# Gate and value by 15 products per 3 x 2 x 3 blocks instead of 7 per 2 x 2 x 2, in a Mamba2 scan with a SwiGLU layer

## The chip, the cores and the metric

One core of a Trainium2 chip runs the whole computation in one launch. The metric is device microseconds of an execution, median of the runs; lower is better. The engines are named as in the profile: PE (TensorE, matrix products; PEld is its weight load), DVE (VectorE), ACT (ScalarE), POOL (GpSimd) and SP (SyncE), whose queue issues nearly all DMAs. Tiles lie in SBUF, or in PSUM where PE writes its products.

## What is computed

A Mamba2 scan over 4 batches x 8 heads x 768 tokens (head width 32, state 16), whose output, as 3072 tokens x 256 features, goes through an RMS norm and a SwiGLU layer with 1536 hidden features. Everything is float32; the weights come as 64-bit floats.

```python
L = np.exp(cum[:, :, :, None] - cum[:, :, None, :]) * causal   # per chunk of 32 tokens
y_intra = np.einsum('bhij,bhjd->bhid', CB * L, xc)
y_inter = np.einsum('bhin,bhnd->bhid', Cc, state) * decay_to_i
...
xn = x / rms * rms_g                 # 3072 x 256
g, val = xn @ w_gate, xn @ w_val     # 256 -> 1536
out = (g / (1 + np.exp(-g)) * val) @ w_out
```

Written as products of 128 x 128 weights with 256 tokens, gate and value are 2 x 12 x 2 x 12 = 576 products; the output projection is half as much.

## The kernel before

The order of all work is written out by hand as one long string of steps; each step (`2:P.7.0` is step `P` of block 2 with arguments 7 and 0) issues a few instructions, every engine takes its instructions in that order, and an engine waits where an input is not there or a buffer is not free. So the string sets both the queues and what is behind a wait.

The tokens are cut into six blocks of 512 (`TB`). For each block the scan runs on pairs of 128-token chunks: B and C are transposed (`turn`, `T`, `Tt`), decays are spread by DMA (`spread`), shifted on DVE (`sub`, L467), exponentiated on ACT and masked on POOL (`ex`, L473 and L475), multiplied with the products of C and B (`g`, `L`), and give `y` with the carried states (`A`, `S`). The decays of the first four pairs are instead made on PE (`mask`, `sums`, L426 to L447). Then come the squares, the norm (`ms`, `rs`, `rb`, `xn`), and the layer.

The weights are brought in 20 pieces (`fetch`) and turned from 64-bit to 32-bit floats by ACT (`pow`) and DVE (`man`, `wt`: L192, L195, L201). All this work lies in the first 100 us, mixed with block 0, of which the first six feature tiles are computed by plain products (L827, L837).

The other gate and value products go by Strassen's scheme in its Winograd form: two feature tiles x two halves of the 256 inputs x two token halves of 256, 7 products instead of 8, for gate and value side by side in one bank. `combine_w` (`sw`, L881) and `combine_x` (`tx`, L888) make the sums of weights and of tokens; `product_gv` (L911) issues the products, 1, 6, 7, 4 onto the bank `gate` and 2, 5, 3 onto `val`; after 1, 6 and 7 ACT takes out the running sum (`take`, L917, tile `p`), and DVE adds it to `val` (`C`, L923, tile `c`). ACT applies SiLU (`silu`, L932) and DVE multiplies by the value (`hid`, L936) into the hidden tile `h`. The order string runs several pairs of feature tiles side by side.

The projection uses the same scheme on `h` and `w_out`: sums of `h` (`s`, `s3`, `s2`, `s4`; L967 to L977), sums of the weights (`two`, L957), products of 128 columns over all six feature pairs (`O`, L1001), `Otake` on ACT, `Oadd` on DVE (L1025, L1028), and the store. Block 0 is projected by plain products of 256 columns (L943).

Of the kernel before, what the change touches and what calls it, by code (L numbers as in the profile page):

```python
# [20 lines left out]
def kernel(  # L21
# [13 lines left out]

# [11 lines left out]
    NPAIR = T // 256  # L66
    TB = 512
    NT = TB // P
    NBLK = T // TB
# [4 lines left out]
    raw = ctx.enter_context(tc.tile_pool(name="raw", bufs=3))  # L74
    ssd = ctx.enter_context(tc.tile_pool(name="ssd", bufs=2))
    cvt = ctx.enter_context(tc.tile_pool(name="cvt", bufs=2))
    nrm = ctx.enter_context(tc.tile_pool(name="nrm", bufs=2))
    ffn = ctx.enter_context(tc.tile_pool(name="ffn", bufs=2))
    mm = ctx.enter_context(tc.tile_pool(name="mm", bufs=1, space=bass.MemoryType.PSUM))
    dram = ctx.enter_context(tc.tile_pool(name="dram", bufs=1, space=bass.MemoryType.DRAM))  # L80
    ctx.enter_context(tc.manual_schedule())
# [20 lines left out]

    pairs, later, sides = {}, {}, ("left", "right")
# [9 lines left out]
    def load(p, queues=(nc.sync, nc.sync)):  # L113
        b, c0 = divmod(2 * p, NC)
        br = raw.tile([P, 2, NH, N], FP32, tag="br", name="br")
        cr = raw.tile([P, 2, NH, N], FP32, tag="cr", name="cr")
        st.setdefault(p, {}).update(B=br, C=cr)
        for i in range(2):
            sl = slice((c0 + i) * P, (c0 + i + 1) * P)
            for dst, src in ((br, B), (cr, C)):  # L120
                queues[i].dma_start(out=dst[:, i], in_=src[b, :, sl, :].rearrange("h s n -> s h n"))  # L121

    def load_x(p, queue=nc.sync):
        b, c0 = divmod(2 * p, NC)
        st.setdefault(p, {})["x"] = raw.tile([P, 2, NH, D], FP32, tag="xr", name="xr")
# [5 lines left out]
    wgv = const.tile([P, 2, 2, DF], FP32, name="wgv")  # L131
    wg, wv = wgv[:, 0], wgv[:, 1]
    wo = const.tile([P, NF, DM], FP32, name="wo")

    def words(w):
# [7 lines left out]
    wdst = {"g": wg, "v": wv, "o": wo}  # L143
    pieces = [(n, c, w) for c, w in [(0, 128), (128, 128)] + [(c, 256) for c in range(256, DF, 256)]
              for n in "gv"]
    pieces += [("o", c, 2) for c in range(0, NF, 2)]
    fetched = {}

    def fetch(*ks):
        for k in ks:  # L150
            n, c, w = pieces[k]
            if n == "o":
                src, dst, shape = wsrc[n][:, c:c + w], wo[:, c:c + w], (w, DM)
            else:
                src, dst = wsrc[n][:, :, 2 * c:2 * (c + w)], wdst[n][:, :, c:c + w]
                shape = (2, w)
            small = shape[0] * shape[1] == 256
            r = raw.tile([P, shape[0], 2 * shape[1]], I32, tag="ws" if small else "wr",
                         name="wr", bufs=4 if small else 6)
# [6 lines left out]

    parts = {}

    def power(k):
        words16, (lo, hi), dst, shape = fetched[k]
        n = shape[1] * shape[2]
        e = cvt.tile([P, n], FP32, tag="e", name="e", bufs=4)
# [10 lines left out]
    def mantissa(k):  # L189
        words16, (lo, hi), dst, shape = fetched[k]  # L190
        m = cvt.tile(shape, I32, tag="m", name="m")
# [6 lines left out]
    def weight(k):  # L198
        words16, (lo, hi), dst, shape = fetched[k]
        e, f = parts.pop((k, "e")), parts.pop((k, "f"))  # L200
        nc.vector.scalar_tensor_tensor(out=dst, in0=f, scalar=2.0 ** -20, in1=e,  # L201
                                       op0=ALU.mult, op1=ALU.mult)

    a_sb = ffn.tile([BH, S], FP32, tag="ob", name="a_sb", bufs=1)
# [25 lines left out]
    early = nrm.tile([P, NC * BH + 2 * NG * NH], FP32, tag="xn", name="early", bufs=1)  # L230
# [128 lines left out]
    def three_parts(k):  # L359
        r_ps = ps.pop(("r", k))  # L360
        first = nrm.tile([P, 2, P], BF16, tag="first", name="first", bufs=1)
        nc.vector.tensor_copy(out=first, in_=r_ps)
        rest = nrm.tile([P, 2, P], FP32, tag="rest", name="rest", bufs=1)
        nc.vector.scalar_tensor_tensor(out=rest, in0=first, scalar=later_part, in1=r_ps,
                                       op0=ALU.mult, op1=ALU.add)
        second = nrm.tile([P, 2, P], BF16, tag="second", name="second", bufs=1)
# [46 lines left out]
    def pair_tile(g):  # L413
        p = g // 2
        if p not in Ls and p < 4:
            Ls[p] = ssd.tile([P, 2, NH, P if p < 2 else HC], FP32, tag="L", name="L", bufs=2)
        elif p not in Ls:
            Ls["of", p // 2] = L = ssd.tile([P, 4, NH, HC], FP32, tag="L", name="L", bufs=2)
            for k in range(2):
                Ls[p - p % 2 + k] = L[:, 2 * k:2 * k + 2]  # L420
# [61 lines left out]
    def scale(p):  # L482
# [3 lines left out]
        for name, src, d in (("Cd", "C", to_i), ("Bd", "B", from_j))[0 if p < 2 else 1:]:  # L486
            s[name] = ssd.tile([P, 2, NH, N], FP32, tag=name, name=name)
# [4 lines left out]
    def transposed(p):  # L492
        s = st[p]
        if "T" not in s:
            s["T"] = ssd.tile([P, 2, 4, P], FP32, tag="T", name="T")
        return s["T"]

# [29 lines left out]
    def spread_decays(p):  # L527
        b, c0 = divmod(2 * p, NC)
        st.setdefault(p, {})["dT"] = d = ssd.tile([P, 2, P], FP32, tag="Cd", name="dT")
# [5 lines left out]
    def turned_decayed(p):  # L535
        nc.vector.tensor_tensor(out=transposed(p)[:, :, 3], in0=ps["t", p][:, 1], in1=st[p]["dT"],
# [9 lines left out]
    def turned_last(p, copy):  # L546
        copy(out=transposed(p)[:, :, 3], in_=ps.pop(("t", p)))
# [31 lines left out]
    def products_of_block(blk, g):  # L579

        ps["g", blk] = gs = [g[:, 0], g[:, 1], bank("g2", (P, 512)), bank("g3", (P, 512))]
        ps["g pair", blk] = g
        for k in range(2):
            product(2 * blk + k, [(q, gs[q][:, 256 * k:256 * k + 256]) for q in range(NQ)], k == 0)

    def decayed_block(blk, q=None):

        L = Ls["of", blk]
        if q is None:
            L = L[:, :, 0:4].rearrange("p j (q t) m -> p q j (t m)", t=2)  # L590
            g = ps["g pair", blk].rearrange("p q (j m) -> p q j m", j=4)
        else:
            L = L[:, :, 2 * q:2 * q + 2].rearrange("p j t m -> p j (t m)")
            g = ps["g", blk][q].rearrange("p (j m) -> p j m", j=4)
# [39 lines left out]
    def states(p):  # L634
        A_ps = ps.pop(("A", p))
        b, c0, chunks = chunks_of(p)
        new = ssd.tile([P, 2, 2, 2, D], FP32, tag="A", name="A")
# [6 lines left out]
        for i, u in chunks:  # L644
            g, c = 2 * p + i, c0 + i
            S = ssd.tile([P, 2, D], FP32, tag="S", name="S", bufs=10)
# [9 lines left out]
    yts, sqs = {}, {}  # L656

    def first_outputs(p, y):
# [4 lines left out]
        def inter(i, opens):  # L663
            S, CdT = state[2 * (2 * p + i) - 1], s["T"][:, i, 3]
# [24 lines left out]
    def outputs(p, pair, after, n=0):  # L689
# [6 lines left out]
        width = 1 if p < 4 else 2  # L696

# [6 lines left out]
        for i in range(2):  # L704
            for u in range(2):
                for q in range(NQ):
                    if (2 * p) % NC == 0 and i == 0 and u == 0:
# [5 lines left out]
                              rhs=s["T"][r, i, 3, halves[u]], tile_position=(32 * q, o))  # L713
# [7 lines left out]
        for k, p2 in enumerate(after):  # L721
            cols = slice((width + n + k) * P, (width + n + k + 1) * P)
            additions(p2, [y[u][:, cols].rearrange("p (i t d) -> p i t d", i=2, t=2)
                           for u in range(2)])
        del st[p], Ls[p]

    def parts_of_y(p):
        y, n = ps["y", p], 2 if p < 4 else 4
# [3 lines left out]

    def squares(p):
        blk, half = divmod(p, 2)
        if half == 0:
            sqs[blk] = nrm.tile([P, TB], FP32, tag="sq", name="sq", bufs=1)
        tk = slice(half * 256, half * 256 + 256) if p < 4 else slice(0, TB)
        if p < 2:
            sq2 = nrm.tile([P, 2, 256], FP32, tag="sq2", name="sq2", bufs=1)
            nc.scalar.activation(out=sq2, in_=ps["y", p][:, :, 0:256], func=AF.Square)  # L740
            nc.gpsimd.tensor_tensor(out=sqs[blk][:, tk], in0=sq2[:, 0], in1=sq2[:, 1], op=ALU.add)
            return
        n, parts = parts_of_y(p)
        sq2 = nrm.tile([P, 2 * n * HC], FP32, tag="sq2", name="sq2", bufs=1)
        for k, us, y in parts:
            dst = (sqs[blk][:, tk], sq2)[k].rearrange("p (j u m) -> p u j m", j=n, u=2)
            nc.scalar.activation(out=dst[:, us],
                                 in_=y.rearrange("p u (j m) -> p u j m", j=n), func=AF.Square)
        nc.gpsimd.tensor_tensor(out=sqs[blk][:, tk], in0=sqs[blk][:, tk], in1=sq2, op=ALU.add)

    def taken_out(p, copy):
        blk, half = divmod(p, 2)
        if half == 0:
            yts[blk] = nrm.tile([P, 2, TB], FP32, tag="yt", name="yt", bufs=1)
        tk = slice(half * 256, half * 256 + 256) if p < 4 else slice(0, TB)
        if p < 2:
# [635 lines left out]
```

## Time and profile before

| | |
|---|---|
| runs, device us | 403.6, 405.26, 405.27; median 405.26 |
| profiled execution, first to last instruction | 402.1 us (no other time of it is given) |
| PE busy | 394.8 us, 98% |
| gate and value by Strassen (L911) | 924 rows, 462 products |
| plain gate and value (L827, L837) | 32 rows of 512 columns, 32 of 256 |
| projection (L1001; L943) | 840 rows of 128 columns; 96 of 256 |
| DVE busy | 297.9 us, 74% |
| ACT busy | 224.5 us, 56% |
| POOL busy | 37.6 us, 9% |
| granted clock of PE | 1.00 from 0 to 380 us, 0.96 in the last stretch |

Each fp32 product stands as two rows of PE, each with its own weight load. A row's end is modelled, so rows of PE that follow each other overlap in the list; their rate is read from a run of many. The slices of the page are 10 us long. "Idle before" is the time an engine sat idle ahead of a group, with what ended it.

### The profile page before, as it was taken

How to read it: one execution, taken by the hardware profiler on the slowest of the kernel's cores; microseconds unless marked ns; L12 is line 12 of the kernel's file. 1: busy time of each engine (PE TensorE's matmuls, PEld its weight loads, DVE VectorE, ACT ScalarE, POOL GpSimd, SP SyncE). 2: the span in 40 equal slices, each digit the busy share in tenths (PEclk: the TensorE clock that was granted, in tenths of full speed). 3: DMA queues.
4: the chain of work that ended last, by engine and by line, in shares of the span. 5: the costliest groups of instructions: out<-in, count | busy, mean ns of one | idle time of the engine just before them, and what ended most of it. 6: DMA issues, size and time to landing. Idle time of an engine off the chain costs nothing.

```text
span 402.1 us, 9591 instructions
## 1 busy us (share of the span) xinstructions
PE 394.8 (98%) x3881; PEld 338.9 (84%) x3881; DVE 297.9 (74%) x686; ACT 224.5 (56%) x456; POOL 37.6 (9%) x57
## 2 busy tenths in 40 slices
PE   8989999999999999999999999999999999999997
PEld 5656477888888899888899988899988899988996
DVE  6999999999477997567689467887555767366871
ACT  3989887894684362753572653482645551445410
POOL 2210010001300021200102300021200010000000
PEclk9999999999999999999999999999999999999999
DMA  9989997129012306301223700202000001100001
GB/s 110 189 248 277 178 183 236 38 42 96 2 39 67 68 22 118 79 0 17 68 74 80 104 2 0 44 30 71 27 2 2 2 9 54 52 0 2 0 2 52
DMA packets 92595, 26.99 MB, mean 67 GB/s; under 512 B 77288, under 2 KB 86376, under 8 KB 92552
## 3 DMA queue, kind: packets, MB, share of 16 engines
q1 hardware_dynamic: 88392, 26.13, 30.1%
q10 hardware_dynamic: 4160, 0.26, 0.8%
q8 instruction: 30, 0.49, 0.5%
q14 instruction: 13, 0.11, 0.1%
HBM read 22.64 MB, written 3.74 MB: 66 GB/s over the span
## 4 chain that ended last, share of the span: by engine, by line
PE 91%; SPq 3%; DMA 2%; DVE 1%; ACT 1%; issue 0%
PE gate L911 28%; PE o L1001 24%; PE val L911 21%; PE o L943 5%; PE gate L827 4%; PE y L699 3%; PE gate L837 2%; PE g L562 2%; SPq L121 1%; DMA wr<-in_moe_w_val_dram 1%; PE tp L505 1%; SPq L128 1%; DMA br<-in_B_dram 1%; PE y L627 1%; SPq L160 1%; PE ms L777 0%
## 5 line engine op out<-in xcount | busy, mean ns | idle before, releaser
L923 DVE TENSOR_TENSOR c<-val,p 128x512 f32<-128x512 f32 x99 | 67.5, 688 | 33.8 <-PE val L911 29.6
L917 ACT COPY p<-gate 128x512 f32<-128x512 f32 x99 | 57.4, 581 | 53.2 <-PE gate L911 50.4
L911 PE MATMUL gate<-tx,sw 128*128 128x256 f32 x264 | 65.8, 381 | 0.0
L932 ACT ACTIVATE c<-c 128x256 f32<-128x256 f32 x99 | 39.5, 416 | 44.5 <-DVE c L923 44.5
L911 PEld LDWEIGHTS gate<-tx,sw 128*128 128x128 f32 x264 | 49.5, 190 | 7.1 <-issue 0.3
L936 DVE TENSOR_TENSOR h<-c 128x256 f32<-128x256 f32 x99 | 41.1, 426 | 18.2 <-ACT c L932 18.2
L911 PE MATMUL val<-xn,sw 128*128 128x256 f32 x132 | 33.6, 382 | 0.5 <-DVE c L923 0.5
L911 PE MATMUL val<-tx,sw 128*128 128x256 f32 x132 | 33.6, 383 | 0.1
L911 PE MATMUL val<-xn,wgv 128*128 128x256 f32 x132 | 33.7, 382 | 0.0
L911 PE MATMUL gate<-xn,wgv 128*128 128x256 f32 x132 | 33.4, 380 | 0.0
L911 PE MATMUL gate<-tx,wgv 128*128 128x256 f32 x132 | 33.0, 381 | 0.0
L475 POOL TENSOR_SCALAR_AFFINE_SELECT L<-L 64x512 f32<-64x512 f32 x32 | 23.7, 740 | 87.0 <-ACT L L473 85.8
L1001 PE MATMUL o<-wo,h 128*128 128x128 f32 x240 | 29.9, 276 | 0.0
L1001 PEld LDWEIGHTS o<-wo,h 128*128 128x128 f32 x240 | 28.5, 192 | 0.5 <-issue 0.2
L1001 PE MATMUL o<-two,h 128*128 128x128 f32 x240 | 28.9, 276 | 0.0
L1001 PE MATMUL o<-two,s 128*128 128x128 f32 x240 | 28.9, 276 | 0.0
L911 PEld LDWEIGHTS val<-xn,sw 128*128 128x128 f32 x132 | 24.8, 190 | 4.2 <-DVE c L923 0.9
L1001 PEld LDWEIGHTS o<-two,s 128*128 128x128 f32 x240 | 28.0, 192 | 0.4 <-issue 0.2
L911 PEld LDWEIGHTS val<-tx,sw 128*128 128x128 f32 x132 | 24.7, 190 | 3.9 <-DVE c L923 0.5
L1001 PEld LDWEIGHTS o<-two,h 128*128 128x128 f32 x240 | 27.8, 192 | 0.2 <-DVE s L967 0.2
L911 PEld LDWEIGHTS gate<-tx,wgv 128*128 128x128 f32 x132 | 24.8, 190 | 3.5 <-ACT c L932 0.2
L911 PEld LDWEIGHTS val<-xn,wgv 128*128 128x128 f32 x132 | 24.8, 190 | 3.5 <-issue 0.2
(188 smaller groups left out, 614.1 us busy)
## 6 DMA issues: line engine op xcount, KB each, us to landing
L<-rowd SPq DMA_DIRECT2D x32, 128.0 KB, 3.0
xr<-in_x_dram SPq DMA_DIRECT2D x24, 128.0 KB, 4.7
wr<-in_moe_w_out_dram SPq DMA_DIRECT2D x6, 512.0 KB, 7.0
wr<-in_moe_w_val_dram SPq DMA_DIRECT2D x5, 512.0 KB, 6.4
wr<-in_moe_w_gate_dram SPq DMA_DIRECT2D x5, 512.0 KB
out_dram<-ob SPq DMA_DIRECT2D x9, 256.0 KB, 2.2
br<-in_B_dram SPq DMA_DIRECT2D x22, 64.0 KB
cr<-in_C_dram SPq DMA_DIRECT2D x22, 64.0 KB, 2.4
```

Of the source, the lines that this page charges most:

```text
L475: nc.gpsimd.affine_select(out=L[r], in_=L[r], pattern=[[0, NH], [1, HC]], compare_op=ALU.is_ge, fill=0.0, base=0, channel_multiplier=-1)
L562: nc.tensor.matmul(out=g[u, P * i:P * i + P].rearrange("p (t m) -> p t m", t=2), lhsT=T[r, i, 0, u], rhs=T[r, i, 1:3, u], start=(first and ...
L699: nc.tensor.matmul(out=y[2 * k + u][rows, (2 * n + i) * HC:(2 * n + i + 1) * HC], start=(k, u, rows.start) not in opened, stop=True, skip_ ...
L827: nc.tensor.matmul(out=gv[:, k], lhsT=w[:, t, fs], rhs=xns[0][:, t], start=(t == 0), stop=(t == 1))
L837: nc.tensor.matmul(out=gv[:, k, tk], lhsT=w[:, t, fs], rhs=yts[0][:, t, tk], start=(s == 0 and t == 0), stop=(t == 1), skip_group_check=True)
L911: nc.tensor.matmul(out=dst[:, half[w]], lhsT=lhsT, rhs=rhs, start=(k in (1, 2, 5) and w == 0), stop=True, skip_group_check=True)
L917: nc.scalar.copy(out=t, in_=Xs[j])
L923: nc.vector.tensor_tensor(out=t, in0=Zs[j], in1=a, op=ALU.add)
L932: nc.scalar.activation(out=u, in_=src[:, half[0]], func=AF.Silu)
L936: nc.vector.tensor_tensor(out=hidden_tile(blk, j)[:, c // 10 - 1, c % 10 - 1], in0=u, in1=src[:, half[1]], op=ALU.mult)
L943: nc.tensor.matmul(out=o, lhsT=hs_[blk, f // 2][:, f % 2, k // 2, (k % 2) * P:(k % 2 + 1) * P], rhs=wo[:, f], start=opens, stop=(f == NF - ...
L1001: nc.tensor.matmul(out=o[t] if apart else o[:, t * P:(t + 1) * P], lhsT=lhsT[:, t], rhs=rhs, start=(k in (1, 2, 4, 5) and j == 0 and (apar ...
```

## The change

Tokens. The six blocks of 512 become four batches of 768, and the work of the layer runs in eight groups `n`: the four batches with the first 768 hidden features (n = 0 to 3), then the four batches again with the other 768 (n = 4 to 7). The first half's projection gives partial results, which go to DRAM (`put_half`, `parted`), are fetched back (`get_half`, step `get`) and are added in when the second half is projected (`before_o`, step `Obef`, on DVE in place of `Otake`).

Products. Gate and value of groups 1 to 7 go by a scheme for 3 x 2 x 3 blocks: three feature tiles x two halves of the inputs x three token thirds of 256, 15 products instead of 18. `combine_u` makes 11 weight tiles for each of the two triples of feature tiles of a half (step `U`), `combine_v` twelve token tiles for each group (`V`). Of the 15 products of a triple twelve accumulate, one after the other, on the bank `gate` (`X`), and three on `val` (`Z`); after each of them the sum so far is read, by ACT (`take`, five of them and a SiLU) or by DVE (`C`, eight of them, and a product). Two triples run side by side. Group 0 has plain products: as before for its first 512 tokens, and `late` for the last 256.

Engines. The steps `U`, `V`, `join`, `hid`, `two`, `s`, `s2`, `s3` and `s4` exist on DVE and, with the letter p, on POOL (`hidp`); the order string chooses: of these, 52 of `hid`, 44 sums of `h`, 36 of `V`, 23 of `U`, 8 of `join` and 3 of `two` go to POOL.

Weights. The pieces of the second half are converted later, written to DRAM (`apart`) and fetched back (`back`) once the scan's buffers are closed (`second_half`, step `half`). Pair 3 has its decays by DMA, not on PE. The order string is the same up to the first gate products, and new from there on.

The core of the diff:

```diff
-    TB = 512
+    TB = S
+    FH = NF // 2
...
+        if k >= FIRST:
+            apart[k] = dram.tile(shape, FP32, name="apart%d" % k)
+            nc.sync.dma_start(out=apart[k], in_=dst)
+
+    def second_half():
+        scans.close()
+        late = ctx.enter_context(tc.tile_pool(name="late", bufs=1))
+        weights.append(half_of_weights(late, 1))
...
+    def combine_u(n, u, k, engine):
+        a, U = weight_parts(u)
+        todo = {0: ("neg", a[31], a[32]), 3: ("sub", a[21], U[0]), 1: ("add", U[3], a[22]),
+                4: ("add", a[11], a[32]), 5: ("sub", a[31], a[11]), 7: ("add", a[11], a[12]),
+                8: ("add", a[21], a[31]), 12: ("add", a[12], a[22]), 13: ("sub", a[12], a[32]),
+                14: ("add", U[12], U[8]), 22: ("add", a[11], a[21]), 2: ("neg", U[2], U[12])}
...
+        Vs[n, k] = t = hold.tile([P, 256], FP32, tag="V", name="V", bufs=12)
+        engine.tensor_tensor(out=t, in0=in0, in1=in1, op=op)
...
+    chain = {13: "X", 11: "X", 4: "X", 10: "X", 5: "X", 8: "X", 6: "X", 3: "X", 0: "X", 1: "X",
+             2: "X", 7: "X", 14: "Z", 12: "Z", 9: "Z"}
...
+        for w in range(2):
+            nc.tensor.matmul(out=dst[:, half[w]], lhsT=lhsT[:, w], rhs=rhs,
+                             start=(k in (13, 14) and w == 0), stop=True, skip_group_check=True)
...
+    def joined_gv(n, t, engine):
+        v = vs[4, n, t]
+        engine.tensor_tensor(out=v, in0=v, in1=vs[14, n, t], op=ALU.add)
...
+        in0, in1 = (Xs[n, t], v)[::-1 if swap else 1]
+        nc.vector.tensor_tensor(out=o, in0=in0, in1=in1, op=ALU.subtract)
...
+        engine.tensor_tensor(out=hidden_tile(n, f // 2)[:, f % 2, c % 10 - 1], in0=u,
+                             in1=src[:, half[1]], op=ALU.mult)
...
+    def before_o(n, k, c):
+        a, m, v, o = cells[c]
+        ts[n, k, c] = v = hold.tile([P, 3, P], FP32, tag="v", name="v", bufs=3)
+        nc.vector.tensor_tensor(out=v, in0=thirds_of(Os[n, "X"]),
+                                in1=before[n, a][:, :, m * P:(m + 1) * P], op=ALU.add)
...
+    for name, fn in (("U", combine_u), ("V", combine_v), ("join", joined_gv), ("hid", hide_gv),
+                     ("two", combine_wo), ("s", combine_h), ("s3", difference_h), ("s2", second_h),
+                     ("s4", fourth_h)):
+        kinds[name], kinds[name + "p"] = on(dv, fn), on(pl, fn)
...
+        s6:P.0.1 s6:C.33.1 s6:P.1.0 s7:P.14.1 s6:P.1.1 s6:silu.33.1 s6:C.23.0 s7:Vp.9 s6:silu.23.0
+        s6:hid.23.0 s6:hidp.31.1 s7:Vp.3 s6:hidp.32.0 s7:P.14.0 s6:C.23.1 s6:P.2.0 s5:Oadd.21
```

## The prediction

> **What bounds the kernel now.** I read the page's first two parts, then a table of busy time by stage, the chain of waits, the groups by shape, and two stretches of the timeline.
>
> ```profile
> PE 394.8 (98%) x3881; PEld 338.9 (84%) x3881; DVE 297.9 (74%) x686; ACT 224.5 (56%) x456; POOL 37.6 (9%) x57
> PE   8989999999999999999999999999999999999997
> DVE  6999999999477997567689467887555767366871
> ```
>
> TensorE (PE) is busy in every slice; VectorE (DVE) too in the first ten. The stages say it more sharply (columns: stretch, its length, busy time and count of PE, PEld, DVE, ACT, POOL, then clock, DMA share, GB/s):
>
> ```profile
> 20.00:60.00 40.00, 38.09 (x450) 23.61 (x447) 38.45 (x85) 35.08 (x62) 2.77 (x3) 1.00 0.93 221
> 60.00:100.00 40.00, 39.48 (x326) 33.20 (x325) 38.08 (x87) 30.88 (x56) 2.47 (x3) 1.00 0.52 106
> 100.00:180.00 80.00, 80.00 (x759) 72.09 (x758) 58.37 (x132) 44.64 (x97) 10.87 (x15) 1.00 0.24 50
> 180.00:390.00 210.00, 210.00 (x2081) 189.90 (x2080) 144.01 (x321) 100.19 (x214) 16.44 (x19) 1.00 0.13 31
> ```
>
> So there are two regimes: from 20 to 100 us PE and DVE are both full (DVE 96%); from 100 to 390 us PE alone is (DVE about 70%, POOL 9%). The chain of waits gives PE's rate where nothing holds it:
>
> ```profile
> 80.05 6.91 PE o L943 x32
> 270.14 11.17 PE o L1001 x100
> 344.94 1.73 PE gate L911 x8
> ```
>
> A 256-column fp32 row costs 1.73/8 = 0.216 us, a 128-column one 11.17/100 = 0.112 us; every fp32 product is two rows. Durations of the other engines (busy in all and mean ns behind the bar):
>
> ```profile
> L923 DVE TENSOR_TENSOR c<-val,p 128x512 f32<-128x512 f32 x99 | 67.5, 688 | 33.8 <-PE val L911 29.6 <-ACT p L917 2.2 <-ACT c L932 0.9
> L936 DVE TENSOR_TENSOR h<-c 128x256 f32<-128x256 f32 x99 | 41.1, 426 | 18.2 <-ACT c L932 18.2
> L749 POOL TENSOR_TENSOR sq<-sq,sq 128x512 f32<-128x512 f32 x4 | 5.4, 1342 | 137.4 <-issue 72.5 <-ACT sq L747 32.7 <-DVE S L651 32.2
> ```
>
> Last, what happens when POOL works beside DVE (timeline: start, length, engine, line, count):
>
> ```profile
> 149.37 1.54 POOL L475 TENSOR_SCALAR_AFFINE_SELECT L<-L 64x512 f32<-64x512 f32 x2 [3.90 <-ACT L L473]
> 149.52 1.66 DVE L974 TENSOR_TENSOR s<-s,h 128x256 f32<-128x256 f32 x2
> ...
> 254.93 1.13 PE L911 MATMUL gate<-tx,sw 128*128 128x256 f32 x4
> 256.10 0.58 ACT L917 COPY p<-gate 128x512 f32<-128x512 f32 x1 [1.14 <-PE gate L911]
> ...
> 262.79 0.69 DVE L923 TENSOR_TENSOR c<-val,p 128x512 f32<-128x512 f32 x1
> 262.92 1.27 POOL L749 TENSOR_TENSOR sq<-sq,sq 128x512 f32<-128x512 f32 x1 [37.83 <-issue]
> 263.40 1.41 DVE L936 TENSOR_TENSOR h<-c 128x256 f32<-128x256 f32 x2
> ```
>
> Two L974 sums, 0.75 us in other places (385.24 us), took 1.66 under two POOL selects. Of the pair at 263.40 the first was held until POOL's end at 264.19. The L923 sum at 262.79, one of whose inputs is the PSUM tile `val`, kept its 0.69. So a DVE operation with all its inputs in SBUF ("SBUF-only" below) and a POOL operation take turns; one that reads PSUM passes.
>
> **The change part by part.** Its counts are those of the changed kernel's instruction listing; the sum is made against the span, 402.1 us. The median of the runs, 405.26, lies 3.2 above that span; I add these 3.2 at the end.
>
> *PE.* Gate and value: 462 Strassen products of 256 columns become 420 (seven groups x 2 x 15 x 2) plus 24 direct ones (`late`): 18 x 2 x 0.216 = 7.8 us less. Projection: 420 products of 128 columns and 48 of 256 become 504 of 128: 840 x 0.112 + 96 x 0.216 = 114.8, after 1008 x 0.112 = 112.9, 1.9 less. Pair 3 now gets its decays by DMA, so two of the four `never` masks, half of the 64x64 sums and four of the eight 64x512 sums go (busy 1.2, 0.9, 0.8 us in all): about 1.3 less. The rest of the scan keeps its counts. PE: -11.0 us, all on the path, as PE bounds both regimes.
>
> *DVE.* Removed: 99 x 0.688 (L923), 132 x 0.42 (L936), 120 x 0.43 (the sums of h), 48 x 0.45 (`sw`, `tx`), 12 x 0.42 (`two`), 22 output sums (8.2), 10 x 0.744 (`xn`): 217 us. Added: 112 x 0.69 (C), 80 x 0.42 (hidden), 52 sums of h of 384 columns at 0.55 (midway between 0.42 and 0.69), 73 x 0.42 (U and V), 5 x 0.55, 6 x 0.69 (join), 48 x 0.55 (Oadd, Obef), 9 for xn and two more subtractions: 213 us. No net load. Nine of the twenty weight pieces, 0.45 + 0.69 + 0.69 = 1.8 us each (L192, L195, L201), move behind the first eleven. I added these durations up along both listings, engine by engine, from where PE has 25 us of listed work to where it has 100: DVE has 72 us there before and 67 after.
>
> *POOL.* Added: 52 hidden, 23 U, 36 V of 256 columns (0.73, the shortest L741 and L749 of that width), 44 sums of h and 3 `two` of 384 (1.0, midway), 8 joins of 512 (1.27): 81 + 47 + 10 = 138 us, from 37.6 to about 176.
>
> *What POOL costs DVE, early.* In the same stretch POOL's listed work rises by 23.5 us, to 26, while 51 of DVE's 67 us are SBUF-only. With DVE always busy each POOL microsecond meets such work three times in four: 17.6 lost, 4.7 saved, 13 us at the most. At the least, POOL works only beside PSUM reads: 51 + 26 = 77 us of turn-taking work must fit PE's 75, 2 us. Six U sums stand in a row on POOL where DVE converts pieces (L188 and L191 of the changed kernel, SBUF-only), so the low end is unlikely; but PE has some lead over DVE. I take +7, with 2 to 13.
>
> *Later.* From 105 us of PE's listed work on, 108 us of the POOL work are new, against 103 SBUF-only us of DVE in a stretch of 282: a chance of 0.37 to meet, 40 us more on DVE's 205, so 245: not yet the bound on average. In one place it is: between 145 and 165 DVE has 20 us, 17 of them SBUF-only, and POOL 11, so 28 us that take turns beside 20 of PE. New, too, is that all but three of the fifteen products of a group accumulate on one bank (`X`), and each is read before the next. The turnaround is 0.17 (a row's modelled end behind its issue: 1.03 for x4 less 4 x 0.216), 0.04 to the reader (254.93 + 1.13 to 256.10), 0.69, 0.04: 0.94 us. The order puts other PE work between: 1.7 us or more ahead of all but one of DVE's reads before the change; after it 16 of the DVE reads have 0.6 to 1.2, and 51 have 1.5 to 1.7. That leaves room for one SBUF-only operation ahead of the read, not for one that waits for POOL. Low end 0 (all of it inside DVE's idle 30%), high end 20 (half of the 40 reaches PE); I take +6, nearer the low end, since most reads of X pass POOL.
>
> *End.* Now the last store is 64 KB behind a 0.29 sum; then 384 KB behind 0.55: +0.26, and +0.7 by the 1.8 us of 128 KB and 2.2 of 256 KB drawn out. The last C, silu and hidden (0.94 + 0.42 + 0.43) have one 0.67 us projection step ahead of them: +1. Together +2 (0.5 to 4).
>
> *Hidden.* 34 new DMAs (9 weight pieces out and back, 8 partial results out and back, 11 MB) run where the DMA share is 0.13 to 0.24. `back` waits on SP for the scan's last reader; behind it stand the stores of s1 and s2 and later `get`, needed a group (about 42 us) later. Were that cover gone: nine pieces at 2.2 us, 20 us. ACT has 84 copies instead of 99: less.
>
> [...]
>
> Sum: 402.1 - 11.0 + 7 + 6 + 2 = 406.1; with 3.2, 409 us.
>
> **The rivals.** (A) The saving stands: PE is full again and only the low ends are paid, 402.1 - 11 + 2 + 2 + 1.5 = 396.6, so 400 us. For it: from 100 us on DVE has 30% idle, and the C reads, which dominate the section of the X bank, pass POOL. Against it: DVE's 96% in the first 100 us. It holds as long as the three terms of loss together stay under 9 us. (B) Gain and loss cancel within 0.5%, 403 to 407 (0.5% is about what a measurement of this kernel can tell from no change). (C) The X bank's turnaround becomes the bound: each of the 112 reads is behind one operation that waits half a 1.0 us POOL turn, 0.25 more than the room (1.6 - 0.94 - 0.42); 28 us instead of 6, 431 us. Against it: the order sets POOL's hidden products beside PSUM reads. (D) That the change does not do what it says: the listing has its 840 + 48 rows; I give this no chance.
>
> **How the numbers follow.** Forecast (407 to 418, point 409): 0.46. A: 0.36, B: 0.10, C: 0.08. Faster 0.36, same 0.10, slower 0.54. The range 396 to 422 leaves out a few hundredths of A's low end and C with the forecast's tail.
>
> **What would show it.** Right: PE's L979 rows still 0.216 us apart inside pairs, but PE idle before `gate` rows with DVE as releaser, most of it before 100 us of work; SBUF-only groups (h<-p, s<-s,h, V) with means well over 0.42 and 0.55, PSUM readers at 0.69; POOL near 180 us or more. Wrong: PE at 98% of a span near 395, or idle PE that ends with a DMA or with ACT.

## The result, and the profile after

The changed kernel takes 454.04 us (median of 4 runs, 452.43 to 455.42), the kernel before 404.68 us beside it: a ratio of 1.122, with an interval of 1.118 to 1.126. The forecast was 409 us with a range to 422. The sign was right, the size was not: the change costs 49 us, where 4 were forecast.

The first two parts of the page of the changed kernel, the busy times and the slices (here 11.3 us each):

```profile
PE 406.4 (90%) x3865; PEld 339.0 (75%) x3865; DVE 336.6 (75%) x632; ACT 217.1 (48%) x423; POOL 187.1 (41%) x225
PE   8986987798987789978999999999899999999994
DVE  7997876779987589975873786774867747866782
PEclk9998898689998999989999999999999999999999
```

TensorE was at 98% of the span and is at 90%. The holes lie in the first half, where its granted clock falls below full speed as well. No other engine is full there in its place. The same stretches as before the change (stretch, length, PE, PEld, DVE, ACT, POOL, clock, DMA share, GB/s):

```profile
20.00:60.00 40.00, 33.03 (x322) 18.94 (x321) 34.26 (x71) 30.09 (x52) 10.00 (x12) 0.91 0.82 182
60.00:100.00 40.00, 31.98 (x568) 24.90 (x566) 28.68 (x57) 30.27 (x49) 16.12 (x19) 0.83 0.64 120
100.00:180.00 80.00, 68.45 (x826) 57.49 (x827) 68.42 (x119) 49.94 (x89) 37.65 (x41) 0.98 0.55 129
180.00:390.00 210.00, 201.05 (x1594) 177.01 (x1593) 149.62 (x264) 79.87 (x175) 98.20 (x115) 0.99 0.14 45
```

DVE was at 96% between 20 and 100 us, and is at 79% there. So the stage that was full before now waits, all engines in turn.

A busy PE at a low clock is not PE at work (between 44 and 51 us it is busy in all 7.00 us, at a clock of 0.65), so I use one measure more, called lost time below: the time passed, less the PE rows issued so far at their durations of full clock (0.216 us for 256 columns, 0.112 for 128, 0.43 for 512, the small tiles of the scan at their pace in the kernel before). It is worked out row by row from the trace:

| stretch of the span, us | lost before | lost after | more |
|---|---|---|---|
| 0 to 20 | 11.0 | 10.7 | -0.3 |
| 20 to 100 | 9.1 | 31.8 | 22.7 |
| 100 to 220 | 3.5 | 30.7 | 27.2 |
| 220 to 31 us ahead of the end | 3.7 | 8.2 | 4.5 |
| the last 31 us | 3.1 | 8.1 | 5.0 |
| span | 402.1 = 371.7 + 30.4 | 451.4 = 361.9 + 89.5 | 59.1 |

The products saved 9.8 us of rows. 59.1 us of waiting were added, 50 of them between 20 and 220 us. From 220 us on, where the scan is done, PE is nearly as full as it was.

The groups of VectorE and GpSimd show the turns that the prediction spoke of (line, engine, operation, tiles, count, then busy and mean ns, idle before):

```profile
L997 DVE TENSOR_TENSOR p<-gate,p 128x512 f32<-128x512 f32 x42 | 28.7, 686 | 8.4 <-PE gate L979 7.7 <-POOL h L1012 0.7
L1012 DVE TENSOR_TENSOR h<-p 128x256 f32<-128x256 f32 x35 | 21.8, 636 | 3.9 <-ACT p L1006 3.9
L677 DVE SCALAR_TENSOR_TENSOR S<-S,fcol,A 128x64 f32<-128x64 f32 x36 | 18.0, 501 | 1.0
...
L1012 POOL TENSOR_TENSOR h<-p 128x256 f32<-128x256 f32 x35 | 27.8, 801 | 57.1 <-ACT p L1006 55.8 <-PE o L1066 1.2
```

The reader of PSUM kept its 0.69 us (0.689 in the median of the 59 L997 sums that overlap a POOL operation, 0.686 of the 53 that don't), the SBUF-only product went from 0.42 to 0.64, the state sums (L677) from 0.28 to 0.50. These waits are plain in the trace. Whether they made the 59 us is another matter, and the runs say that most of it they did not.

When is a batch's scan done? Its last step is the sum that makes the normed tokens. The instructions that write `xn` in the kernel before, then in the changed one (count, least, median and most ns, first and last start):

```profile
L804 DVE SCALAR_TENSOR_TENSOR xn<-yt,gcol,r x10: 737/744/748, 94.0 to 338.9; 128x512 f32<-128x512 f32 x10
```

```profile
L839 DVE SCALAR_TENSOR_TENSOR xn<-xn,gcol,r x8: 478/1008/1012, 62.7 to 226.1; 128x768 f32<-128x768 f32 x6, 128x256 f32<-128x256 f32 x2
```

Before, the last tokens were normed at 339 us, block after block of 512 (two instructions each, 0.7 us apart) in steps of 61 us ((338.9 - 0.7 - 94.0) / 4). Now at 226 us, since the first feature half of all four batches comes before any of the second. Batches 1 to 3 are normed at 109, 167 and 225 us, 58 us for 768 tokens. Beside each stands one group of 768 tokens with half the features, 120 rows of 256 columns and 126 of 128, 25.9 + 14.1 = 40 us of PE, and 7 of the scan's own (21.4 for three batches). PE can use 768 tokens every 47 us; it gets them every 58.

PE stands still in places, and the profile names what ended each wait (what waited, for what, us in total, times, longest). The first three are the longest of the changed kernel, the fourth is the wait for normed tokens:

```profile
PE g L587 <- ACT T L1177: 7.4, 5, 4.2
PE gate L979 <- DVE h L1012: 4.8, 3, 2.8
PE y L723 <- issue: 3.6, 3, 1.6
PE gate L979 <- DVE xn L839: 1.7, 2, 1.5
```

Only 1.7 us end with normed tokens. Of the 40 us in the whole list some 20 lie in front of the scan's own products (`g`, `y`, `tp`, `ms`, `A_ps`): PE's rows stand in one queue in the order of the string, so the rows of the group behind such a product wait as well. In the gap at 39.7 us the next `gate` rows, whose weights were made by 38.3 us, start behind `g`, at 44.91 us. The rest of the lost time is the low clock and what this list does not name.

### The profile page after: what moved, and what is told of

It is laid out like the page before. It is cut to its first block, busy times and chain, and to the rows that moved or that the text cites. A ratio compares the mean times of both kernels' runs of the same rounds, so it can differ in the third digit from the quotient of the medians.

```text
span 451.4 us, 9717 instructions
## 1 busy us (share of the span) xinstructions
PE 406.4 (90%) x3865; PEld 339.0 (75%) x3865; DVE 336.6 (75%) x632; ACT 217.1 (48%) x423; POOL 187.1 (41%) x225
## 4 chain that ended last, share of the span: by engine, by line
PE 55%; DVE 21%; ACT 6%; issue 5%; POOL 3%; DMA 2%; SPq 1%; DVEq 0%; ACTq 0%; POOLq 0%
PE gate L979 23%; PE o L1066 17%; PE val L979 5%; PE y L723 3%; DVE h L1012 3%; PE gate L857 3%; DVE S L677 2%; PE g L587 2%; DVE V L959 2%; DVE p L997 2%; DVE ob L1091 1%; DVE L L486 1%; DVE s L1033 1%; ACT T L1177 1%; DMA wr<-in_moe_w_out_dram 1%
## 5 line engine op out<-in xcount | busy, mean ns | idle before, releaser
L979 PE MATMUL gate<-V,u 128*128 128x256 f32 x336 | 84.1, 387 | 0.6 <-DVE p L997 0.3
L979 PEld LDWEIGHTS gate<-V,u 128*128 128x128 f32 x336 | 61.3, 191 | 10.7 <-DVE p L997 1.5
L1012 POOL TENSOR_TENSOR h<-p 128x256 f32<-128x256 f32 x35 | 27.8, 801 | 57.1 <-ACT p L1006 55.8
L979 PE MATMUL gate<-xn,u 128*128 128x256 f32 x168 | 43.6, 393 | 7.9 <-DVE h L1012 4.8
L979 PE MATMUL gate<-V,wgv 128*128 128x256 f32 x168 | 42.8, 382 | 1.0 <-DVE c L997 0.8
L979 PEld LDWEIGHTS gate<-xn,u 128*128 128x128 f32 x168 | 30.4, 192 | 15.0 <-DVE h L1012 5.0
L984 ACT COPY p<-gate 128x512 f32<-128x512 f32 x42 | 24.1, 585 | 36.4 <-PE gate L979 36.4
L997 DVE TENSOR_TENSOR p<-gate,p 128x512 f32<-128x512 f32 x42 | 28.7, 686 | 8.4 <-PE gate L979 7.7
L979 PEld LDWEIGHTS gate<-V,wgv 128*128 128x128 f32 x168 | 30.1, 190 | 5.3 <-DVE c L997 1.2
L997 DVE TENSOR_TENSOR p<-p,gate 128x512 f32<-128x512 f32 x28 | 19.1, 686 | 17.2 <-PE gate L979 14.9
L979 PE MATMUL val<-V,u 128*128 128x256 f32 x112 | 28.8, 381 | 0.4 <-DVE V L959 0.4
```

What stands on the lines that cost most here:

```text
L979: nc.tensor.matmul(out=dst[:, half[w]], lhsT=lhsT[:, w], rhs=rhs, start=(k in (13, 14) and w == 0), stop=True, skip_group_check=True)
L984: nc.scalar.copy(out=v, in_=(Xs if chain[k] == "X" else Zs)[n, t])
L997: nc.vector.tensor_tensor(out=o, in0=in0, in1=in1, op=ALU.subtract)
L1012: engine.tensor_tensor(out=hidden_tile(n, f // 2)[:, f % 2, c % 10 - 1], in0=u, in1=src[:, half[1]], op=ALU.mult)
```

## The experiments

Three theories went into them. T, the prediction's own: POOL and DVE take turns. C: PE's gaps lower its clock, and that makes the loss. S (at first called O): the outer halves leave each scanned token only half of the other work to hide behind, so that the scan's chain of dependent steps sets the pace. Forms of the last name one place each: A is ACT's queue, Q the issue queue of SP, S1 the length of the scan's own chain, S2 the scan's steps standing in queues behind the groups' work. Each time is of one execution, that of the last run is a median of four; the kernel before took 403 to 405 us beside them.

**Without POOL's new work**, or with all of it on DVE:

```diff
-        kinds[name], kinds[name + "p"] = on(dv, fn), on(pl, fn)
+        kinds[name], kinds[name + "p"] = on(dv, fn), on(FirstColumn(), fn)   # e1_first_column
+        kinds[name], kinds[name + "p"] = on(dv, fn), on(dv, fn)              # e1_no_pool
```

> The 138 elementwise steps that the change gave to POOL now write a constant (tiles that are new) and compute one column only: the rest of their results is left out. Order, dependencies and DVE's own work stay. Theory T (POOL and DVE taking turns cost most of the time that was lost before 220 us): 40 us or more come back, 405 to 415 us, and DVE's SBUF-only groups fall to 0.42 (256 columns), 0.55 (384) and the state sums to 0.28. Theory O (late transfers, in-order queues and the scan's chain of latencies leave PE without work, and the turns are a part of it): under 20 us come back, 434 us or more, with the PE gap at 39 us still there.

441.2 us, in the range of theory O. The turns of these steps are gone. The groups of VectorE in this run:

```profile
L677 DVE SCALAR_TENSOR_TENSOR S<-S,fcol,A 128x64 f32<-128x64 f32 x36 | 14.4, 399 | 1.0
L1012 DVE TENSOR_TENSOR h<-p 128x256 f32<-128x256 f32 x35 | 14.3, 421 | 4.5 <-ACT p L1006 4.5
L1033 DVE TENSOR_TENSOR s<-h 128x384 f32<-128x384 f32 x17 | 9.4, 555 | 0.6
```

The products are back at 0.42, and 0.555 is what a sum of 384 columns takes alone (0.55 had been estimated, 0.765 it took in the changed kernel). Only 13 us came back, and POOL's own steps are shorter in this run too, so 13 us is the most that their turns can have cost. At 100 us the lost time is 43.5, against 42.5 in the changed kernel: in the stretch where the prediction put its largest term, these turns cost nothing. Theory T falls as the main cause.

> The same 138 steps run on DVE, nothing is left out; DVE gets about 138 x 0.47 = 65 us of work and loses its waits for POOL. Theory T: the turns were worth about as much as the work, so the early stage gains and the later one loses little: 435 to 450 us. Theory O: DVE's queue gets longer ahead of the scan's steps: 458 to 480 us.

484.9 us, 31 slower, and a little above theory O's range. Of the two places for this work POOL is the better one, turns and all.

**Early order, and the clock.** At 39 us PE has its longest gap. Its causes in the timeline of the changed kernel (start, length, engine, what, and the idle time before with its releaser):

```profile
36.07 3.60 PE L857 MATMUL gate<-xn,wgv 128*128 128x512 f32 x8
...
40.56 0.86 DVE L188 TENSOR_SCALAR m<-wr 128x512 int32<-128x512 int32 x1 [2.27 <-DMA wr<-in_moe_w_out_dram]
...
43.81 1.16 PE L587 MATMUL g<-T 32*64 32x128 f32 x32 [4.15 <-ACT T L1177]
...
44.91 3.78 PE L857 MATMUL gate<-xn,wgv 128*128 128x512 f32 x4
```

A weight piece lands late, DVE waits for it in order, behind it stand the decays of the scan, then ACT, then PE. After the gap four rows of 512 columns take 3.78 us; before it eight took 3.60. So the gap seems to cost its 4 us and then half of PE's speed for a while (rows 0.85 us apart, 0.43 before). Two runs go at this:

```diff
-0:fetch.9 0:rs.0 b1:bc.2 ... b1:x.0 0:fetch.10 0:wt.7 0:man.10 s0:Up.0.5 0:silu.1 0:Td.2 0:Tt.2.0 0:Tt.2.1
+0:fetch.9 0:fetch.10 0:rs.0 b1:bc.2 ... b1:x.0 0:wt.7 s0:Up.0.5 0:silu.1 0:Td.2 0:Tt.2.0 0:Tt.2.1 0:man.10
```

> The fetch of weight piece 10 goes ahead of the six transfers of batch 1 on SP, and its conversion on DVE behind the decays of pair 2. Theory O: the PE gap of 4.3 us at 39 us goes, and the 4 us in which the granted clock was 0.63 after it: 446 to 450 us. Theory T: within 1.5 us of 454.

453.2 us: a miss for theory O in this form. The gap is gone (0.6 us are left of it, and one of 1.9 stands at 45 us), but at 100 us the lost time is 42.3, as without the edit.

```diff
-0:gg.2/1 ... b1:A ... b1:turn.1 ... b1:g.0 ... b1:turn.2 ... b1:y.0 ... b2:g.0
+0:gg.2*38/1 ... b1:A*14 ... b1:turn.1*16 ... b1:g.0*4 ... b1:turn.2*6 ... b1:y.0*10 ... b2:g.0*18
```

> 96 more bf16 products of 256 columns (0.11 us each at full clock) on TensorE, into PSUM tiles that are about to be written, at seven places where PE waited: 38 ahead of the 4.3 us gap, 4 to 18 at the others. Theory C (PE's gaps lower the granted clock, and the low clock costs more than the gaps): the clock is 0.95 or more in 40 to 48, 72 to 96 and 136 to 144 us, and the time is 442 to 449 us. If what ends the waits is late whatever PE does (T or O alone): the clock may return, but the time stays at 452 to 456.

452.8 us. A stretch of the changed kernel:

```profile
40.00:48.00 8.00, 4.19 (x36) 2.27 (x37) 6.77 (x13) 4.95 (x9) 3.14 (x4) 0.63 0.76 156
```

Two stretches of this run:

```profile
40.00:48.00 8.00, 6.69 (x72) 4.69 (x71) 5.46 (x11) 3.81 (x7) 2.75 (x5) 1.00 0.88 188
60.00:100.00 40.00, 30.97 (x605) 25.21 (x605) 26.11 (x55) 28.00 (x46) 14.75 (x19) 0.96 0.59 117
```

The clock is back (1.00 from 0.63 between 40 and 48 us, 0.96 from 0.83 between 60 and 100), and the time is not; theory C had asked for 442 to 449 us. The fillers are 10.4 us of PE work that costs nothing: PE has that much to spare, and the low clock only filled idle time. Theory C falls. What paces these stretches is not PE.

**Without the scan.** All steps of the scans of batches 1 to 3 are taken out:

```diff
     def thirds(n):
-        xn = xns[n % NB]
+        xn = xns[0]
...
-  every step b1:..., b2:..., b3:... of the order string
```

> Everything of the scans of batches 1 to 3 is left out (loads, turns, states, outputs, norms); all eight groups work on batch 0's normed tokens, with every product, sum, weight piece and store of gate, value and projection as in the changed kernel. The left-out PE work is 21 us at full clock. Theory S (the outer halves give each batch's scan only half of the gate and value work to hide behind, and the scan's chain sets the pace from 60 to 220 us): TensorE's lost time after 60 us falls from about 61 to under 20, 385 to 398 us. If the groups themselves lose it (turns, the X bank, the weights): 415 to 433 us, the 21 us and little more.

401.6 us, 52 faster: the 21 us of rows left out and 31 of waiting. That is a little short of theory S's range, and far outside the other. Lost time from 60 to 220 us falls from 49.4 to 20.1; from 60 us to the end it falls from about 60 to about 35, where theory S asked for under 20. So half of the added waiting is there because of the scan, and the other half is not explained by it.

Next, single places in the scan's chain. ACT's table loads:

```diff
-        nc.scalar.activation(out=u, in_=src[:, half[0]], func=AF.Silu)
+        nc.scalar.activation(out=u, in_=src[:, half[0]], func=AF.Exp)
...
-  the steps table and exps of the order string
```

> Silu is replaced by Exp everywhere and the table preloads are left out, so ACT loads its table once and not 23 times (16 of them, 20 us of ACT, between 25 and 140 us; the kernel before has 7 there). Theory A (ACT's queue, with its table loads, is the scan chain's slowest part): 435 to 444 us. Theory S with DVE, SP and transfers as the chain: 447 to 454 us.

450.2 us, in the range of theory S and not of A: 28 us of ACT (22 table loads of 1.28 us) are worth 4 us. The weight pieces of the second half, whose conversion shares the queues:

```diff
     def mantissa(k):
+        if k >= FIRST:
+            nc.gpsimd.memset(f, 0.0)
+            nc.vector.tensor_scalar(out=m[:, :, 0:1], in0=hi[:, :, 0:1], scalar1=0xFFFFF,
+                                    scalar2=0x100000, op0=ALU.bitwise_and, op1=ALU.bitwise_or)
+            return
...
```

> The conversion of the nine weight pieces of the second half is left out but for a first column (27 operations each on ACT and DVE, about 20 us on each); their fetches, stores and loads stay. Theory S: they stand in the same queues as the scan's steps, 8 to 15 us come back, 439 to 446 us. Theory T (only the turns with POOL): within 4 us of 454.

455.2 us: no gain, theory S's number missed. Nothing in the whole kernel waits for this conversion long enough to show. The issue queue of the broadcasts:

```diff
     def spread(g):
-            nc.sync.dma_start(out=pair_tile(g)[r].rearrange("p h m -> p (h m)"), ...
+            nc.gpsimd.dma_start(out=pair_tile(g)[r].rearrange("p h m -> p (h m)"), ...
```

> The 36 broadcasts of row decays into the L tiles (0.6 us of SP each) are issued by POOL and not by SP. Theory Q (SP's one queue, in which they stand ahead of loads and weight fetches, sets the scan's pace): 438 to 447 us. If it does not: 451 to 460 us, the upper end by POOL's own steps behind them.

465.7 us, worse than either range. POOL spends 36 x 0.54 us on the issues, and its own steps stand behind them in its queue. The run gives no sign that SP is the cause; as it loads POOL instead, it doesn't rule it out either.

So no single place does it. Is the chain as a whole too long?

```diff
-  every step s1:..., s2:..., s3:... of the order string
...
-        nc.sync.dma_start(out=before[n, a], in_=parted[n - NB, a])
+        nc.sync.dma_start(out=before[n, a], in_=parted[0, a])
```

> The groups s1 to s3 (the first feature half of batches 1 to 3) are left out with all their products, sums and stores; the scans of batches 1 to 3 keep their order and dependencies, and the second half reads group s0's partial results for all. Their PE work is 3 x 40 = 120 us at full clock. Theory S1 (the scan's own chain of latencies is nearly as long as the period of 58 us from one normed batch to the next): the normed tokens come every 40 to 55 us, and the time falls by less than 60 us, to 394 to 430 us. Theory S2 (the scan's steps are late because they queue behind the groups' work on DVE, ACT and POOL): every 20 to 35 us, 310 to 370 us.

404.1 us, with the normed tokens at 110, 154 and 207 us: 44 and 52 us for a batch, though 120 us of PE work beside it are gone. It is the number that S1 asked for. But PE has little to do here and its clock is low: 0.57 in the mean from 100 to 220 us, with PE busy in 43.1 of these 120 us, and 0.50 in this stretch of the run:

```profile
120.00:140.00 20.00, 10.20 (x318) 8.17 (x319) 11.75 (x22) 10.41 (x18) 7.38 (x11) 0.50 0.67 126
```

At 0.50 the scan's 7 us of rows for a batch would take 14, so by this estimate up to 7 of the 44 and of the 52 us can be the clock's. The chain of waits from 111 to 156 us in this run shows why (start, length, engine, tile and line; only some of its pieces):

```profile
117.66 0.30 DVE S L677
...
121.07 2.00 DMA apart<-m
...
123.08 0.64 POOL L L494
...
126.63 0.69 DVE L L621
...
131.14 0.48 ACT T L1177
131.66 1.26 PE g L587 x32
...
134.19 2.89 PE y L723 x109
...
139.69 2.98 DMA L<-rowd
142.70 0.88 ACT sq L769 x2
143.71 1.81 POOL sq L771
145.57 0.91 PE ms L804 x8
...
147.34 3.30 DMA roots<-r
```

States, masks, transposes, `g`, `y`, squares, norm, DRAM and back: one after the other on PE, DVE, ACT, POOL and the DMA, 45 us during which each of them does little. (A converted weight piece on its way to DRAM, `apart<-m`, stands in the chain too.) The broadcast `L<-rowd` of the next batch comes only after `y`, as there is a single L tile; a second one was not tried.

At 47 us a batch the tokens of batches 2 and 3 would be wanted at 156 and 203 us. Alone the scan has them at 154 and 207, so its chain has little time to spare; in the whole kernel they come at 167 and 225. The step from the one to the other comes of running beside the groups, in the same queues.

One link of the chain alone, the norm's way through DRAM:

```diff
     def spread_roots(b):
-                in_=roots[b].rearrange("t q m -> q t m"))
+                in_=rowe[0:32, 0:TB].rearrange("q (t m) -> q t m", t=4))
```

> The norm's roots of batches 1 to 3 are still computed and stored, but the tile that scales the tokens is loaded from a tensor that is long complete: the wait for sums, Ln, Exp, store and load back (about 10 us of each batch's 58) is left out. Theory S1 (latency of the scan's chain): 6 to 10 us for each of three batches, 424 to 436 us. Theory S2 (queues): 449 to 455 us.

454.3 us, S2's number. In the whole kernel the normed tokens of batch 2 come at 167 us, and at 168 without the wait for the hop. In both runs the sum on DVE stands directly behind the hidden products and sums of h of the group before, which end at 167 and at 168 us. The chain of the scan and that of the group are woven into the same queues; here, shortening one shows the other.

The masks, which are POOL's own old work:

```diff
         nc.scalar.activation(out=L, in_=L, func=AF.Exp)
-        for r in halves:
-            nc.gpsimd.affine_select(out=L[r], in_=L[r], ...
```

> The 36 selects of POOL on the L tiles of batches 1 to 3 (0.74 us each, in the kernel before too) are left out. Beside them the state sums take 0.69 us, 0.31 in the kernel before. If these turns are on the scan's chain: the sums fall to 0.3 and 6 to 12 us come back, 442 to 448 us. If not: the sums fall, the time stays at 452 to 456 us.

445.2 us, as expected if these turns are on the scan's chain. The median state sum falls from 0.508 to 0.285 us. So there are such turns, and they are not those of the new steps alone: in the kernel before the same selects stood elsewhere than beside the state sums (0.285 there), now they stand beside them. The normed tokens of batch 3 come 9 us earlier, as does the end. The edit also spares the chain the selects' own time.

Do the prices add? Two runs join two of the diffs above: the scan and POOL's new steps left out, then the masks and POOL's new steps.

> Both leavings-out together: the scans of batches 1 to 3, and all but a constant and one column of POOL's new steps. If the turns' price (13 us alone) adds to the scan's (31 us of waiting, 21 of work): 386 to 391 us. If the two are one wait counted twice: 395 to 402 us. What TensorE still loses after 60 us is then neither: 10 to 18 us.

391.1 us, 10.5 less than without the scan alone: the two prices add nearly in full. The lost time left, 48.8 us, is still 18 more than before the change; some 25 of it lie behind 60 us, where 10 to 18 had been expected.

> POOL's selects on L are left out and its 138 new steps cut to a constant and one column, so that nearly nothing takes turns with DVE. If the two prices add: 454 - 13 - 9 = 432 us, and the rest of the loss is the scan's chain. If the turns hide behind one another: 437 to 441 us. Had the turns been the cause: 405 to 415 us.

436.3 us: 18 of the 22 us. Nearly without any turns the kernel still loses 72.7 us to waiting, 42 more than the kernel before. That settles theory T as the main cause: it asked for 405 to 415 us.

**The kernel before, with half the work beside its scan.** The test of theory S from the other side:

```diff
-  of blocks 1 to 4, in the steps P, take, C, silu, hid, s, s2, s3, s4 and O, those of feature pairs 3, 4 and 5
```

> The kernel before with half of blocks 1 to 4's features left out (three of six feature pairs: products, sums, projections), so that each scanned block of 512 tokens has half of the gate, value and projection work beside it. Left out are 4 x 27.6 = 110 us of TensorE at full clock. Theory S (half of the work can't cover a scan, whatever the kernel): the normed blocks come every 40 us or more, where 60 us was the pace, and the time is 320 to 350 us. If the old scan keeps up (the loss is made by the new scan's form, 768 tokens at once and single buffers): every 32 to 35 us, 294 to 305 us.

340.0 us, in theory S's range, where TensorE's own work would have allowed 294. The stretch where the scans run, and the normed tokens:

```profile
100.00:220.00 120.00, 97.83 (x1143) 82.34 (x1141) 79.12 (x176) 55.55 (x122) 19.48 (x24) 0.93 0.29 62
```

```profile
L804 DVE SCALAR_TENSOR_TENSOR xn<-yt,gcol,r x10: 737/744/751, 95.0 to 278.3; 128x512 f32<-128x512 f32 x10
```

A block every 46 us ((278.3 - 0.7 - 95.0) / 4), where full PE would have taken 61 - 27.6 = 33. The kernel loses 46 us to waiting that it did not lose with full work, at a lowered clock too, with DVE at 66% and POOL at 16%: the picture of the changed kernel without its new scheme, and with POOL doing little. The order string was written for the full work, though, and only had steps taken out; one written for half the work was not tried.

```diff
+            for again in range(2 if n in (1, 2, 3) and k in (13, 11, 4, 10, 5, 8) else 1):
                 nc.tensor.matmul(out=dst[:, half[w]], lhsT=lhsT[:, w], rhs=rhs, ...
```

> Six of the fifteen products of the groups s1 to s3 are issued twice: 72 more products of 256 columns, 31 us of TensorE at full clock between 109 and 260 us. Theory S (TensorE waits for the scan there): 465 us or less, at most a third of the 31 us is paid. If TensorE's own work sets the pace: 478 to 486 us.

473.6 us: 19.5 of the 31 us are paid, between the two ranges, so theory S's number is missed. Part of the reason is in the run. A third of the repeats, 10.4 us, belongs to the group of batch 3, which runs behind the scan where PE has no slack. Of the 20.7 us beside the scan, 11.5 fit into PE's waits; the rest delays what stands behind it in PE's queue, the scan's own products too: the normed tokens of batches 2 and 3 come 5 and 9 us later.

```diff
-  b1:S.0 ... b1:S.1 b1:ex.0 b1:S.2 ... b2:S.0 b2:S.1 b2:sub.5 s1:V.6 s1:Vp.8 b2:S.2
+  b1:S.0 b1:S.1 b1:S.2 ... b1:ex.0 ... b2:S.0 b2:S.1 b2:S.2 b2:sub.5 s1:V.6 s1:Vp.8
```

> Nothing is left out. The fetch of piece 10 comes earlier and its conversion later, as in e1_fetch_order, and the state sums of batches 1 and 2 stand together on DVE, ahead of the selects of their L tiles. If a better order of a few steps shortens the scan's chain: 444 to 450 us. If not: 452 to 456 us.

Ratio 1.129 to the kernel before (1.123 to 1.136), median 458.2 us: no gain from another place for a few steps. A wholly new order was not tried. No complete version here beats the kernel before.

**One number across the runs.** The work behind the scan is about the same in the changed kernel and in eight of the runs (`e1_fetch_order`, `e1_fillers`, `e2_one_table`, `e2_no_convert`, `e2_spread_pool`, `e3_no_hop`, `e3_no_select`, `e4_order`). In all nine the span ends 225 to 227 us after the last tokens are normed: 226.1 of 451.4 us in the changed kernel, 217.4 of 443.4 without the masks, 236.9 of 464.0 with the broadcasts on POOL. Nearly all of their differences in time arise before the scan ends. Where POOL's new steps are cut too, it is 219 to 220 us, so some 5 of their 13 us lie behind the scan.

## Why the prediction was wrong

**PE, -11.0 us.** Right but for a little: the rows of the two spans differ by 9.8 us.

**"What POOL costs DVE, early", +7.** This is the step that failed. Between 20 and 100 us 22.7 us were lost, and the turns that the term priced cost nothing there (43.5 us lost without them, 42.5 with). The arithmetic of the turns was sound, and so was the finding that DVE's listed work hardly changes (72 against 67 us). What lost the time there is in good part the scan: without the scans of batches 1 to 3 the lost time between 60 and 100 us falls from 18.7 to 5.9. The error was to take a stage's pace from the sum of work on its busiest engine. The prediction counted what was moved on each engine and not how soon the scan's results are now wanted, so the wait for the scan stood in its sum at nothing. It could have been had from the rows: the old scan gave 512 tokens in 61 us; the new order wants 768 in 47 (40 of a group's rows, 7 of the scan's), twice the pace, from a chain that passes through four engines, DMAs and DRAM. With half the work beside it even the old scan gave a block only every 46 us, and the new scan alone takes 44 to 52, with PE at a mean clock of 0.57.

**"Later", +6 (0 to 20).** The mechanism is there, and its size lies inside the range: taking POOL's new steps out gave 13 us, all behind 100 us. But the loss from 100 us to the last 31 us of the span is 31.7 us above the kernel before, and the scan explains more of it than the turns: without the scans of batches 1 to 3 the lost time of 100 to 220 us falls from 30.7 to 14.2.

**"End", +2 (0.5 to 4).** 5.0 us were lost more in the last 31 us, a little over the range. By the term's own figures (1.8 us for 128 KB, 2.2 for 256, so 0.4 for each 128 KB) the longer last store is an estimated 1.0 us and not 0.7; the output stores of 384 KB took 2.7 us in the median.

**"Hidden", 0.** The conversion of the second half's pieces gave nothing back when left out, so no loss is seen from it. The loads of the pieces (`back`) fall after 220 us, where PE is full.

**The rivals**, by the prediction's letters. A and B needed PE full again; it is at 90%. C, the turnaround of the X bank, gave a time nearer to the result, but by the wrong cause: once the scan is done, the groups, with twelve of their fifteen products on that bank, run with 8.2 us lost in 200 (the kernel before lost 3.7 in the 151 us that answer to them), and its reads keep their 0.69 us. The rival that was missing is the scan's pace. Of the signs that were to show the prediction right, the slow SBUF-only groups, the readers of PSUM at 0.69 us and POOL at 187 us came. PE's idle time ahead of `gate` rows with DVE as releaser did not come as told: it is some 9 us, all of it behind 100 us. And a sign of being wrong came: PE's longest idle time ends with ACT (7.4 us ahead of `g`).

**What stays open.** Of 59 us, about 30 go with the scan's waiting and about 17 with turns (89.5 us lost, 72.7 with nearly no turns); the scan's share has some of the turns in it, since the selects stand beside its sums. With both the scan and the new steps out, 18 us are left. About 10 of these lie between 20 and 100 us, where the last third of batch 0 waits for its own scan (PE ahead of `late`, 4.2 us in one gap of the run without scans); no run separates the rest. What makes the scan late in the whole kernel is open as well: its own chain is about as long as the time it has, and which shared queue, or which places in the order, make the last tokens some 19 us later than alone, no run tells.

## What to carry to other kernels

Before a change of loop order, ask of each producer chain how soon its results will be wanted, and compare that with the length of the chain, and not only with the load of its engines. Work that is hidden is hidden behind something: the outer halves took away half of the cover, and a chain that had cost nothing came to set the pace. When a gap is closed or the clock is brought back and the time does not move, the late thing is elsewhere; take the whole producer out to see how much hangs on it.

## What the runs showed of the hardware

In the changed kernel PE stood still for 4.15 us (39.7 to 43.8 us), and its granted clock was 0.63 in the mean between 40 and 48 us. Rows of 512 columns started 0.43 us apart ahead of the gap and 0.85 behind it (45.9 to 48.5 us); they are 0.43 us apart again from 49.1 us, 5.3 us after PE took up work. With the gaps filled (`e1_fillers`) the clock was 1.00 between 40 and 48 us, and the time 452.8 us against 454.04, since what was waited for came no sooner.

A state sum on DVE (L677, 64 columns) takes 0.285 us where no POOL operation overlaps it (13 of 36), and 0.68 in the median of the 21 beside POOL's selects of 64 partitions x 512, which take 0.74 in the mean: 0.40 us more, over half of such a select. In the kernel before none of the 36 overlaps one. Yet in the whole the turns made DVE's busy time 44 us longer (336.6, and 293.0 where nearly all are gone), and the kernel 18: DVE had idle time for the rest.
